# Attention for one query per head over 16 heads: a pair's maximum and exponentials between two Ks, three transfers joined, spare products ahead of every V

## The chip, the core and the metric

The kernel runs on one core of a Trainium2 chip. The metric is device time in microseconds (us). Three runs of the kernel before took 316.85, 317.12 and 317.5 us; their median is 317.12 us. The engines are named as in the profile: PE (matrix products), PEld (its weight loads), DVE (vector), ACT (scalar functions), POOL (GpSimd) and SP, which issues nearly all transfers here.

## The reference

```python
B, H, Sq, Sk, D = 1, 16, 1, 8192, 256          # q, k, v in bfloat16

def reference(q, k, v):
    scale = q.shape[-1] ** -0.5
    scores = jnp.einsum("bhqd,bhkd->bhqk", q, k) * scale
    p = _softmax(scores, axis=-1)
    return jnp.einsum("bhqk,bhkd->bhqd", p, v)
```

There is one query row for each head, so K and V (67 MB each) are read once and used once. The output is 16 rows of 256 numbers.

## The kernel before

**Tiles.** The heads are taken two at a time, as eight pairs, 0 to 7. K of a pair is a tile of 128 partitions (64 for each head) with 128 keys of 256 numbers in each partition, 8.39 MB; V of a pair has the same form. `kbuf` holds two Ks, `vbuf` one V. K5, say, is the K of pair 5. A "side" is one half of a K, 64 keys in each partition (`SIDES`, `HJ`).

**The order of the transfers** is written out by hand in `ORDER` and issued by SP in one queue (L138). A name with `+` is the second part of a K (keys 64 to 127) or of a V (from key 70, `VC`). V7 comes in five pieces (`CUTS`). Ahead of a K, SP waits until DVE and POOL are done with the K two before it (semaphores `kd` and `tp`). Ahead of a V, or of a part from key 70, it waits until PE is done with all of the V before (`pr`), and ahead of a V's first part until PE is done with the first 70 keys of the V before (`pa`). A wait on SP holds everything behind it in the list.

**Scores.** In each side, POOL multiplies 24 of the 64 keys by the query, three keys at a time ("a group", L215), into one of two buffers `prod`; ACT sums each group (L452) and thereby frees the buffer. DVE multiplies and sums the other 40 keys by itself (L252). A K has 16 groups, eight in each side. Semaphore `tp` counts groups multiplied, `sp` groups summed (it starts at 2).

**Maximum and exponentials.** `top` (L234, DVE) takes the maximum of a pair's scores in each partition, `turned` (L292, PE) turns it into a row, `xmax` (L238, DVE) takes the maximum of each head, `spread` (L295, PE) hands it to all partitions, and `expo` (L406 and L411, ACT) makes the exponentials `E`. In the kernel before, DVE and ACT do this for pair h-1 after the first side of pair h (`s == 0`), and at the end, for pair 7, after its last side.

**V.** PE then multiplies E with V, two keys in one product (`doubles`, L317): 35 products for keys 0 to 69, 29 for the rest; for V7, 14 products for keys 70 to 97 and 60 small ones (L386) for the last 30 keys, as they land. `total` (L305) sums the exponentials. ACT copies the sums out (`collect`, L425), PE gathers the parts (`gather`, L342), ACT divides and writes them (`final`, L432). Each round h of PE's loop does V of pair h-1 first, then `turned` and `spread` of pair h, then `gather` of pair h-1. `keep_running` (L331) makes 12 products whose result nobody uses; before, it stands behind `spread` in rounds 6 and 7, in place of the query product that the other rounds have there.

What the change touches, and what calls it:

Of the kernel before, what the change touches and what calls it, by code (L numbers as in the profile page):

```python
# [6 lines left out]
ACT = mybir.ActivationFunctionType  # L7
# [5 lines left out]
NPL = 24  # L13
GRP = 3
CH = 8
SIDES = 2
ORDER = "k0 k0+ k1 v0 k2 v1 k3 v2 k4 v3 k5 v4 k6 k6+ k7 v5 v5+ k7+ v6 v6+ v7"
CUTS = (0, 70, 98, 114, 124)
LAST_PAIRED = 98
SPARES = 6  # L20
STRIP = 64
BLK = 32
ROWS = 98
AHEAD = {"sp": 2, "fin": 1, "rc": 2, "pr": 2, "pv": 2}


def bass_standalone__mha_softmax__decode_kernel(nc: bass.Bass, q: bass.AP, k: bass.AP, v: bass.AP, out: bass.AP):
    B, H, Sq, D = q.shape
# [23 lines left out]
    with contextlib.ExitStack() as ctx:  # L52
# [46 lines left out]
        spare = ps("spare", [P, 512])  # L99

        stream = []
        parts = {name: (0, HJ if name[0] == "k" else VC) for name in ("k0", "k6", "k7", "v5", "v6")}
        for name in ORDER.split():
            kind, n = name[0], int(name[1])
            if name == f"v{LAST}":
                for a, b in zip(CUTS, CUTS[1:] + (J,)):
                    stream.append((kind, n, a, b, "v" if a < VC else "vb" if a < LP else f"w{a}"))
            elif name.endswith("+"):
                stream.append((kind, n, HJ if kind == "k" else VC, J, "vb" if kind == "v" else "k7b" if n == LAST else "kb"))
            else:  # L110
                stream.append((kind, n, *parts.get(name, (0, J)), f"k{n % 2}" if kind == "k" else "v"))

# [10 lines left out]
        @(lambda f: f(nc.sync))  # L123
        def _(sp):
            for kind, n, a, b, name in stream:
                if kind == "k" and n >= 2 and a == 0:
                    sp.wait_ge(sem("kd"), (n - 1) * NC)
                    sp.wait_ge(sem("tp"), (n - 1) * NG)
                elif kind == "v" and n >= 1 and a in (0, VC):
                    sp.wait_ge(*((sem("pa"), n) if b <= VC else (sem("pr"), n + 2)))  # L130
                if kind == "k" and n == 0 and a == HJ:
                    for late in ("k1", "kb", "k7b", "vb"):
                        sp.nop().then_inc(sem(late), 16)
                if kind == "k":
                    buf = kbuf[:, n % 2 * J * D :]
                else:
                    buf = vbuf
                sp.dma_start(buf[:, a * D : b * D], src(k if kind == "k" else v, n)[:, a * D : b * D]).then_inc(  # L138
                    sem(name), 16
                )  # L140
            sp.wait_ge(sem(stream[-1][-1]), 16)
            sp.wait_ge(sem("fin"), LAST + 1)
            flat = out.rearrange("b (n two) s d -> two (b n s) d", two=2)
            rows = qo[:, :].rearrange("t (n d) -> t n d", d=D)
            sp.dma_start(flat[:, 0:LAST, :], rows[:, 0:LAST, :]).then_inc(sem("o"), 16)
            sp.wait_ge(sem("fin"), LAST + 3)
            sp.dma_start(flat[:, LAST:NP, :], rows[:, LAST:NP, :]).then_inc(sem("o"), 16)
            sp.wait_ge(sem("o"), 32)
            sp.nop()
# [4 lines left out]
            e.wait_ge(sem("k1"), (h + 1) // 2 * 16 + 16)  # L154

        def side_wait(e, h, s):
            side, sides = h * SIDES + s, NP * SIDES
            e.wait_ge(sem("kb"), ((side + sides - 1) // sides + (side + 3) // sides) * 16 + 16)  # L158
            e.wait_ge(sem("k7b"), (side + 1) // sides * 16 + 16)

        @(lambda f: f(nc.gpsimd))
        def _(pool):
# [42 lines left out]

            with pool.Fori(0, NP) as h:
                par = pool.snap(h % 2)
                with pool.Fori(0, SIDES) as s:
                    k_waits(pool, h)
                    side_wait(pool, h, s)  # L210
                    pool.nop().then_inc(sem("turn"), 1)
                    with pool.Fori(0, SG // 2) as i:  # L212
                        for b in range(2):
                            pool.wait_ge(sem("sp"), h * NG + s * SG + i * 2 + (b + 1))  # L214
                            pool.tensor_tensor(  # L215
                                out=prod[:, b * GRP * D : (b + 1) * GRP * D].rearrange("p (b d) -> p b d", b=GRP),
                                in0=kbuf[
                                    :, ds(par * (J * D) + s * (HJ * D) + i * (2 * GRP * D) + b * (GRP * D), GRP * D)
                                ].rearrange("p (b d) -> p b d", b=GRP),
                                in1=q_now[:, ds(par * D, D)].rearrange("p (b d) -> p b d", b=1).to_broadcast([P, GRP, D]),  # L220
                                op=ALU.mult,
                            ).then_inc(sem("tp"), 1)

        @(lambda f: f(nc.vector))
        def _(dve):
# [15 lines left out]

            with dve.Fori(0, NP + 1) as h:
                par = dve.snap(h % 2)
                with dve.Fori(0, SIDES) as s:
                    with dve.If(h < NP):
                        k_waits(dve, h)
                        side_wait(dve, h, s)
                        dve.nop().then_inc(sem("turn"), 1)
                        with dve.Fori(0, SC) as c:
                            for b in range(CH):  # L250
                                col = kbuf[:, ds(par * (J * D) + s * (HJ * D) + c * (CH * D) + (NPL + b) * D, D)]
                                ins = dve.scalar_tensor_tensor(  # L252
                                    out=col,
                                    in0=col,
                                    scalar=SCALE,
                                    in1=qrow[:, ds(par * 512, D)],
                                    op0=ALU.mult,
                                    op1=ALU.mult,
                                    accum_out=S[:, ds(par * J + s * HJ + c * CH + (NPL + b), 1)],
                                )  # L260
                            ins.then_inc(sem("kd"), 1)
                    with dve.If(s == 0):
                        with dve.If(h > 0):
                            top(h, 1)
                            xmax(h, 1)
                        with dve.If(h > 1):
                            recips(h, 2)
            recips(NP, 1)
            dve.wait_ge(sem("pv"), NP + 3)
            dve.wait_ge(sem("rc"), NP + 2)  # L270
# [10 lines left out]
        def _(pe):  # L281
# [75 lines left out]
            with pe.Fori(0, NP + 1) as h:  # L357
                par = pe.snap(h % 2)
                with pe.If(h > 0):
                    pe.wait_ge(sem("ex"), h)  # L360
                    pe.wait_ge(sem("v"), h * 16)
                    doubles(0, VC).then_inc(sem("pa"), 1)
                    pe.wait_ge(sem("vb"), (h // (NP - 2) + h // LAST + h // NP) * 16 + 16)
                    doubles(VC, LP)
                    with pe.If(h < NP):
                        doubles(LP, J)
                    total(h)
                with pe.If(h < NP):
# [3 lines left out]
                    spread()  # L372
                    with pe.If(h < NP - 2):
                        qcast(back(h, -2), par)
                    with pe.Else():
                        keep_running()
                with pe.If(h > 0):
                    pe.wait_ge(sem("cm"), h)
                    pe.wait_ge(sem("fin"), h)
# [17 lines left out]
        def _(act):  # L397
# [45 lines left out]
            with act.Fori(0, NP + 1) as h:  # L443
                par = act.snap(h % 2)
                other = act.snap((h + 1) % 2)
                with act.Fori(0, SIDES) as s:
                    with act.If(h < NP):
                        with act.Fori(0, SG) as i:  # L448
                            act.wait_ge(sem("tp"), h * NG + s * SG + i + 1)
                            for b in range(GRP):  # L450
                                part = prod[:, ds(i % 2 * (GRP * D) + b * D, D)]
                                ins = act.activation(  # L452
                                    out=part,
                                    in_=part,
                                    func=ACT.Copy,
                                    scale=SCALE,
                                    accum_out=S[:, ds(par * J + s * HJ + i * GRP + b, 1)],
                                )
                            ins.then_inc(sem("sp"), 1)
                    with act.If(s == 0):  # L460
                        with act.If(h > 0):
                            expo(h, 1)
                        with act.If(h < LAST):
                            q_copy(h + 1, other)
                        with act.If(h > 1):
                            collect(h, 2)
                    with act.If(s == 1):
                        with act.If(h > 1):
                            final(h, 2)
            collect(NP, 1)  # L470
            act.wait_ge(sem("pv"), NP + 3)
            act.wait_ge(sem("rc"), NP + 2)
# [32 lines left out]
```

## Time and profile before

| what | us |
|---|---|
| median of three runs | 317.12 |
| the profiled execution, its own time | 317.33 |
| its span (first to last instruction) | 315.9 |
| DVE, POOL, ACT, PE busy | 225.6, 209.5, 194.6, 97.5 |
| share of 16 transfer engines' span in use by SP's queue | 98.8% |

The span is what the page and all views of the trace show. The execution's own time is 1.43 us longer, for what lies around the span. Times in the views count from the start of the span. "Waits" and "chain" rows give a start, a length and the engine and line; a timeline row gives start, length, engine, line, operation, `out<-in`, how many instructions were merged, and in brackets the idle time ahead of it and who ended it.

### The profile page before, as it was taken

What the parts mean: (1) busy time and instruction counts of PE and PEld (TensorE: products, weight loads), DVE (VectorE), ACT (ScalarE), POOL (GpSimd) and SP (SyncE); (2) the same over time, 40 slices, a digit from 0 to 9 for tenths busy, and PEclk for the clock granted to TensorE, in tenths of its full rate; (3) what the DMA queues carried; (4) which work ended last, traced back from release to release, by engine and by line L of the source; (5) the groups of instructions that cost most, each with busy time, mean ns of one, the idle gap of its engine ahead of it and who ended that gap; (6) DMA issues with size and microseconds to landing.
All of it is one profiled execution on the core that took longest, in us unless ns stands there. A gap on an engine that the chain in (4) does not pass through costs nothing.

```text
span 315.9 us, 7077 instructions
## 1 busy us (share of the span) xinstructions
PE 97.5 (31%) x701; PEld 45.5 (14%) x701; DVE 225.6 (71%) x1305; ACT 194.6 (62%) x840; POOL 209.5 (66%) x145
## 2 busy tenths in 40 slices
PE   0000000191003900048000490005700355285796
PEld 0000000041001400014000240002300122032344
DVE  0198989695596936969279692896989698969300
ACT  2066677766368653696437964468677967686541
POOL 3188888865586836858368582786888588868300
PEclk9999999997555885559755587555965558759599
DMA  8999999999999999999999999999999999999996
GB/s 333 415 448 465 465 398 398 523 407 398 398 523 407 398 398 498 432 398 398 506 423 398 398 514 415 398 398 465 398 465 398 436 446 446 411 436 421 437 429 260
DMA packets 3640, 134.26 MB, mean 425 GB/s; under 512 B 406, under 2 KB 438, under 8 KB 694
## 3 DMA queue, kind: packets, MB, share of 16 engines
q1 hardware_dynamic: 3620, 134.23, 98.8%
q8 instruction: 1, 0.02, 0.0%
q14 instruction: 1, 0.01, 0.0%
q10 hardware_dynamic: 18, 0.01, 0.0%
HBM read 134.23 MB, written 0.01 MB: 425 GB/s over the span
## 4 chain that ended last, share of the span: by engine, by line
DMA 54%; POOL 16%; ACT 10%; issue 6%; ACTq 6%; PE 4%; POOLq 3%; SPq 0%
DMA kbuf<-in_k_dram 32%; DMA vbuf<-in_v_dram 22%; POOL prod L215 16%; ACT prod L452 8%; ACTq L452 4%; PE acc L317 3%; POOLq L215 2%; ACTq L448 2%; SPq L138 0%; ACT E L411 0%; ACT comb L425 0%; PE ob L386 0%; POOLq L214 0%; POOLq L158 0%; POOLq L212 0%
## 5 line engine op out<-in xcount | busy, mean ns | idle before, releaser
L252 DVE SCALAR_TENSOR_TENSOR kbuf<-kbuf,qrow x640 | 219.9, 417 | 65.1 <-issue 65.1
L215 POOL TENSOR_TENSOR prod<-kbuf,q_now 128x768 f32 x128 | 207.0, 1639 | 83.6 <-ACT prod L452 46.3
L452 ACT ACTIVATE prod<-prod x384 | 155.3, 405 | 103.6 <-POOL prod L215 86.6
L317 PE MATMUL acc<-vbuf,E 128*64 128x512 bf16 x497 | 70.4, 448 | 17.5 <-DMA vbuf<-in_v_dram 14.5
L452 ACT ACTIVATION_READ_ACCUMULATOR prod<-prod x384 | 71.6, 186 | 0.0
L292 PE MATMUL mx<-ident,small 128*1 128x128 f32 x16 | 4.5, 380 | 176.7 <-DVE small L234 176.7
L252 DVE DVE_READ_ACCUMULATOR kbuf<-kbuf,qrow x640 | 52.8, 83 | 0.0
L317 PEld LDWEIGHTS acc<-vbuf,E 128*64 128x64 bf16 x497 | 32.2, 129 | 55.0 <-issue 21.1
L292 PEld LDWEIGHTS mx<-ident,small 128*1 128x1 f32 x16 | 0.7, 81 | 178.1 <-DVE small L234 177.9
L411 ACT ACTIVATE E<-S,negb 64x128 bf16 x16 | 13.8, 864 | 1.6 <-ACT negb L406 1.4
L342 PE MATMUL ob<-comb,small 98*2 98x128 f32 x64 | 6.9, 356 | 16.8 <-ACT comb L425 16.7
L228 DVE RECIPROCAL small<-tot 34x1 f32 (+1 forms) x8 | 1.3, 159 | 9.7 <-PE tot L305 9.6
L238 DVE TENSOR_REDUCE small<-mx 1x2 f32<-1x128 f32 x8 | 2.2, 279 | 8.3 <-PE mx L292 8.3
L411 ACT ACTIVATION_READ_ACCUMULATOR E<-S,negb 64x1 f32 x16 | 7.9, 493 | 0.0
L425 ACT ACTIVATE comb<-acc 98x512 f32<-98x512 f32 x8 | 4.7, 593 | 5.0 <-PE tot L305 5.0
L331 PE MATMUL spare<-ident 128*128 128x512 bf16 x24 | 7.6, 486 | 0.0
L342 PEld LDWEIGHTS ob<-comb,small 98*2 98x2 f32 x64 | 2.6, 96 | 20.2 <-ACT comb L425 18.9
L432 ACT ACTIVATE qo<-ob,small 2x128 f32 x14 | 4.9, 352 | 1.0 <-PE ob L342 0.9
L295 PE MATMUL mx<-small 1*128 1x2 f32 x16 | 4.4, 344 | 3.0 <-DVE small L238 3.0
L295 PEld LDWEIGHTS mx<-small 1*128 1x128 f32 x16 | 3.8, 289 | 6.8 <-DVE small L238 6.8
L234 DVE TENSOR_REDUCE small<-S 128x1 f32 x8 | 2.3, 282 | 2.8 <-ACT prod L452 2.8
L406 ACT ACTIVATE negb<-mx 128x2 f32<-128x2 f32 x8 | 1.3, 166 | 4.3 <-PE mx L295 4.2
(25 smaller groups left out, 21.4 us busy)
## 6 DMA issues: line engine op xcount, KB each, us to landing
kbuf<-in_k_dram SPq DMA_DIRECT2D x6, 4096.0 KB, 27.9
vbuf<-in_v_dram SPq DMA_DIRECT2D x3, 4480.0 KB, 23.6
vbuf<-in_v_dram SPq DMA_DIRECT2D x2, 3712.0 KB, 28.9
vbuf<-in_v_dram SPq DMA_DIRECT2D x1, 1792.0 KB, 8.6
vbuf<-in_v_dram SPq DMA_DIRECT2D x1, 1024.0 KB, 10.7
vbuf<-in_v_dram SPq DMA_DIRECT2D x1, 640.0 KB, 11.8
vbuf<-in_v_dram SPq DMA_DIRECT2D x1, 256.0 KB, 11.9
kbuf<-in_k_dram SPq DMA_DIRECT2D x5, 43.5
```

Of the source, the lines that this page charges most:

```text
L215: pool.tensor_tensor(out=prod[:, b * GRP * D : (b + 1) * GRP * D].rearrange("p (b d) -> p b d", b=GRP), in0=kbuf[:, ds(par * (J * D) + s * ...
L252: ins = dve.scalar_tensor_tensor(out=col, in0=col, scalar=SCALE, in1=qrow[:, ds(par * 512, D)], op0=ALU.mult, op1=ALU.mult, accum_out=S[:, ...
L292: pe.matmul(mx[0:1, 0:P], lhsT=m[:, :], rhs=ident[:, :], start=True, stop=True).then_inc(sem("mT"), 1)
L295: pe.matmul(sm, lhsT=ones[0:1, :].to_broadcast([1, P]), rhs=g[:, :], start=True, stop=True,).then_inc(sem("bc"), 1)
L317: ins = pe.matmul(acc[at : at + STRIP, :], lhsT=E[:, x : x + STRIP], rhs=vbuf[:, j * D : (j + 2) * D], start=(j < 4), stop=(j >= J - 4), s ...
L331: pe.matmul(spare[:, :].rearrange("p (b x) -> p b x", x=2 * P), lhsT=flat[:, n * P : (n + 1) * P], rhs=flat.rearrange("p (b x) -> p b x", ...
L342: ins = pe.matmul(ob[row : row + 2, 0:HW], lhsT=sel[:, 2 * n : 2 * n + 2], rhs=comb[:, n * D + a : n * D + a + HW], start=(n == 0), stop=( ...
L411: ins = act.activation(out=E[rows, 0 : 2 * J].rearrange("p (b two i t) -> p b i two t", b=J // BLK, two=2, t=2)[:, :, :, :, x], in_=S[rows ...
L425: act.activation(out=comb[:, :], in_=acc[0:ROWS, :], func=ACT.Copy).then_inc(sem("cm"), 1)
L432: ins = act.activation(out=qo[:, ds(i * D + a, HW)], in_=ob[row : row + 2, 0:HW], func=ACT.Copy, scale=recip[row : row + 2, ds(i, 1)],)
L448: with act.Fori(0, SG) as i:
L452: ins = act.activation(out=part, in_=part, func=ACT.Copy, scale=SCALE, accum_out=S[:, ds(par * J + s * HJ + i * GRP + b, 1)],)
```

## The change

Four things are done. **The transfers:** K0, K6 and V5 come whole and V5 comes ahead of K7's first part; 22 input transfers of K and V stand in place of 25. **The maximum and the exponentials** of pair h-1 are taken by DVE and ACT before their first instruction on K of pair h, in the place where one K ends and the next begins; `collect` of pair h-2 goes ahead of it on ACT. ACT's loop over 16 groups is one loop now. **The spare products** leave their place behind `spread` and go to the head of every round of PE that has a V: PE waits until the pair's groups are all summed (for V6 in round 7: until five groups of K7 are), makes 12 spare products, and then waits for the exponentials and for V. **POOL and DVE** wait for K once in each pair and only for K7's second part in between.

```diff
-ORDER = "k0 k0+ k1 v0 k2 v1 k3 v2 k4 v3 k5 v4 k6 k6+ k7 v5 v5+ k7+ v6 v6+ v7"
+ORDER = "k0 k1 v0 k2 v1 k3 v2 k4 v3 k5 v4 k6 v5 k7 k7+ v6 v6+ v7"
...
+SPARES_AT = 5
...
-        parts = {name: (0, HJ if name[0] == "k" else VC) for name in ("k0", "k6", "k7", "v5", "v6")}
+        parts = {name: (0, HJ if name[0] == "k" else VC) for name in ("k7", "v6")}
...
             with dve.Fori(0, NP + 1) as h:
                 par = dve.snap(h % 2)
-                with dve.Fori(0, SIDES) as s:
-                    with dve.If(h < NP):
-                        k_waits(dve, h)
+                with dve.If(h > 0):
+                    top(h, 1)
+                    xmax(h, 1)
+                with dve.If(h > 1):
+                    recips(h, 2)
+                with dve.If(h < NP):
+                    k_waits(dve, h)
+                    dve.nop().then_inc(sem("turn"), 1)
+                    with dve.Fori(0, SIDES) as s:
                         side_wait(dve, h, s)
...
-                    with dve.If(s == 0):
-                        with dve.If(h > 0):
-                            top(h, 1)
-                            xmax(h, 1)
-                        with dve.If(h > 1):
-                            recips(h, 2)
...
                 with pe.If(h > 0):
+                    pe.wait_ge(sem("sp"), h * NG + h % NP // LAST * SPARES_AT + AHEAD["sp"])
+                    pe.nop().then_inc(sem("turn"), 1)
+                    keep_running()
                     pe.wait_ge(sem("ex"), h)
                     pe.wait_ge(sem("v"), h * 16)
...
                     with pe.If(h < NP - 2):
                         qcast(back(h, -2), par)
-                    with pe.Else():
-                        keep_running()
...
                 other = act.snap((h + 1) % 2)
...
+                with act.If(h > 1):
+                    collect(h, 2)
+                with act.If(h > 0):
+                    expo(h, 1)
+                with act.If(h < LAST):
+                    q_copy(h + 1, other)
+                with act.If(h < NP):
+                    with act.Fori(0, NG) as i:
+                        first = act.snap(par * J + i // SG * (HJ - NPL) + i * GRP)
+                        act.wait_ge(sem("tp"), h * NG + i + 1)
...
+                with act.If(h > 1):
+                    final(h, 2)
```

How SP's list reads around K6 and K7. Of the kernel before (128x16384 is one half of a K, 128x17920 the first 70 keys of a V, 128x14848 the rest):

```order
L138 DMA vbuf<-in_v_dram 128x32768 [waits pr]
L138 DMA kbuf<-in_k_dram 128x16384 [waits tp,kd]
L138 DMA kbuf<-in_k_dram 128x16384
L138 DMA kbuf<-in_k_dram 128x16384 [waits tp,kd]
L138 DMA vbuf<-in_v_dram 128x17920 [waits pa]
L138 DMA vbuf<-in_v_dram 128x14848 [waits pr]
L138 DMA kbuf<-in_k_dram 128x16384
```

And of the changed kernel, from V4 to V6:

```order
L136 DMA vbuf<-in_v_dram 128x32768 [waits pr]
L136 DMA kbuf<-in_k_dram 128x32768 [waits tp,kd]
L136 DMA vbuf<-in_v_dram 128x32768 [waits pr]
L136 DMA kbuf<-in_k_dram 128x16384 [waits tp,kd]
L136 DMA kbuf<-in_k_dram 128x16384
L136 DMA vbuf<-in_v_dram 128x17920 [waits pa]
```

K6's two halves have become one transfer, V5's two parts one that waits for all of V4, and K7's two halves now follow each other behind V5.

How one round of PE reads from `spread` to `gather`, before:

```order
L295 MATMUL mx<-small 128x2 [waits g]
L373 COMPARE_AND_BRANCH
L283 ISA x2
L283 MATMUL qrow<-qo,which 128x256
L373 UNCONDITIONAL_BRANCH
L329 UNCONDITIONAL_BRANCH
L331 MATMUL spare<-ident 128x512 x2
L329 REGISTER_ALU
L329 COMPARE_AND_BRANCH
L375 UNCONDITIONAL_BRANCH
L377 COMPARE_AND_BRANCH
L342 MATMUL ob<-comb,small 2x128 [waits fin,cm]
```

And from its head to V's second part in the changed kernel:

```order
L359 COMPARE_AND_BRANCH
L360 ISA
L329 UNCONDITIONAL_BRANCH [waits sp]
L331 MATMUL spare<-ident 128x512 x2
L329 REGISTER_ALU
L329 COMPARE_AND_BRANCH
L317 MATMUL acc<-vbuf,E 64x512 [waits v,ex]
L317 MATMUL acc<-vbuf,E 64x512 x34
L366 ISA
L317 MATMUL acc<-vbuf,E 64x512 [waits vb]
```

The spare products (a loop of six rounds with two products) have gone from between `spread` and `gather` to ahead of the first product with V, behind a wait for `sp`; in the last round, that of V7, they come after `spread` of pair 7 and `gather` of pair 6.

More of the change, by code (lines that the diff above doesn't have):

```diff
@@ L108, in bass_standalone__mha_softmax__decode_kernel @@
             elif name.endswith("+"):
-                stream.append((kind, n, HJ if kind == "k" else VC, J, "vb" if kind == "v" else "k7b" if n == LAST else "kb"))
+                stream.append((kind, n, HJ if kind == "k" else VC, J, f"{kind}b"))
             else:
@@ L130, in _ @@
                     sp.wait_ge(*((sem("pa"), n) if b <= VC else (sem("pr"), n + 2)))
-                if kind == "k" and n == 0 and a == HJ:
-                    for late in ("k1", "kb", "k7b", "vb"):
-                        sp.nop().then_inc(sem(late), 16)
                 if kind == "k":
@@ L140, in _ @@
                 )
+                if kind == "k" and n == 0:
+                    for late in ("k1", "kb", "vb"):
+                        sp.nop().then_inc(sem(late), 16)
             sp.wait_ge(sem(stream[-1][-1]), 16)
@@ L156, in side_wait @@
         def side_wait(e, h, s):
-            side, sides = h * SIDES + s, NP * SIDES
-            e.wait_ge(sem("kb"), ((side + sides - 1) // sides + (side + 3) // sides) * 16 + 16)
-            e.wait_ge(sem("k7b"), (side + 1) // sides * 16 + 16)
+            e.wait_ge(sem("kb"), (h * SIDES + s + 1) // (NP * SIDES) * 16 + 16)
         @(lambda f: f(nc.gpsimd))
@@ L207, in _ @@
                 par = pool.snap(h % 2)
+                k_waits(pool, h)
+                pool.nop().then_inc(sem("turn"), 1)
                 with pool.Fori(0, SIDES) as s:
-                    k_waits(pool, h)
                     side_wait(pool, h, s)
@@ L362, in _ @@
                     doubles(0, VC).then_inc(sem("pa"), 1)
-                    pe.wait_ge(sem("vb"), (h // (NP - 2) + h // LAST + h // NP) * 16 + 16)
+                    pe.wait_ge(sem("vb"), (h // LAST + h // NP) * 16 + 16)
                     doubles(VC, LP)
@@ L445, in _ @@
                 other = act.snap((h + 1) % 2)
[L446 to L469, printed above, removed]
+                with act.If(h > 1):
[8 more added lines that the diff above has]
+                        act.wait_ge(sem("tp"), h * NG + i + 1)
+                        for b in range(GRP):
+                            part = prod[:, ds(i % 2 * (GRP * D) + b * D, D)]
+                            ins = act.activation(
+                                out=part,
+                                in_=part,
+                                func=ACT.Copy,
+                                scale=SCALE,
+                                accum_out=S[:, ds(first + b, 1)],
+                            )
+                        ins.then_inc(sem("sp"), 1)
+                with act.If(h > 1):
+                    final(h, 2)
             collect(NP, 1)
```

## The prediction

> **What bounds the kernel now.** I read the page first, then the chain of waits, then the timeline of the last 40 us by engine. The page says that the transfer queue is in use all the time:
>
> ```profile
> span 315.9 us, 7077 instructions
> DMA  8999999999999999999999999999999999999996
> q1 hardware_dynamic: 3620, 134.23, 98.8%
> ```
>
> The chain of waits (start, length, what) gives the landings:
>
> ```profile
> 0.74 12.23 DMA kbuf<-in_k_dram
> ...
> 75.98 43.52 DMA kbuf<-in_k_dram
> ...
> 152.62 44.60 DMA kbuf<-in_k_dram
> 197.24 0.23 POOLq L158
> ...
> 198.52 1.63 POOL prod L215
> ...
> 231.18 33.95 DMA vbuf<-in_v_dram
> ...
> 270.33 23.94 DMA vbuf<-in_v_dram
> 294.32 6.04 PE acc L317 x28
> ...
> 301.47 11.78 DMA vbuf<-in_v_dram
> ```
>
> K0's first half lands at 12.97, K3 at 119.50, K5 at 197.22, V5's second part at 265.13, V6's at 294.27, the last piece but one of V7 at 313.25. Between K3 and K5 lie four whole tiles in 77.72 us, 19.43 us each. So the stream never stops, and the middle of the kernel can't go faster unless the stream does. What ends the kernel is read from the tail of PE's timeline:
>
> ```profile
> 277.20 0.59 PE L292 MATMUL mx<-ident,small 128*1 128x128 f32 x2 [6.91 <-DVE small L234]
> 278.15 0.58 PE L295 MATMUL mx<-small 1*128 1x2 f32 x2 [0.37 <-DVE small L238]
> 278.67 4.89 PE L331 MATMUL spare<-ident 128*128 128x512 bf16 x12
> ...
> 285.50 4.07 PE L317 MATMUL acc<-vbuf,E 128*64 128x512 bf16 x35 [1.40 <-DMA vbuf<-in_v_dram]
> 294.32 6.25 PE L317 MATMUL acc<-vbuf,E 128*64 128x512 bf16 x29 [4.75 <-DMA vbuf<-in_v_dram]
> ...
> 300.50 0.38 PE L292 MATMUL mx<-ident,small 128*1 128x128 f32 x2
> 301.25 0.38 PE L295 MATMUL mx<-small 1*128 1x2 f32 x2 [0.37 <-DVE small L238]
> 301.61 2.75 PE L331 MATMUL spare<-ident 128*128 128x512 bf16 x12
> 304.45 0.61 PE L342 MATMUL ob<-comb,small 98*2 98x128 f32 x8
> 305.14 5.79 PE L317 MATMUL acc<-vbuf,E 128*64 128x512 bf16 x49
> ...
> 311.65 0.60 PE L342 MATMUL ob<-comb,small 98*2 98x128 f32 x8 [0.69 <-ACT comb L425]
> 312.08 2.23 PE L386 MATMUL ob<-vbuf,E 128*2 128x128 bf16 x60
> ```
>
> V7's first 70 keys land 70/128 of 19.43 us after V6, at 294.27 + 10.63 = 304.90, and PE begins V7 at 305.14, having worked without a stop since 300.50. Its last product ends at 314.31, 1.06 us after V7's last piece but one (the last, 4 of 128 keys, lands 0.61 behind that, at 313.86): PE and the stream end together, and PE has no slack from `turned` (300.50) on. What PE waited for there is seen on DVE and ACT:
>
> ```profile
> 297.10 0.29 DVE L234 TENSOR_REDUCE small<-S 128x1 f32 x1 [2.79 <-ACT prod L452]
> 300.92 0.28 DVE L238 TENSOR_REDUCE small<-mx 1x2 f32<-1x128 f32 x1 [3.54 <-PE mx L292]
> ```
>
> ```profile
> 296.71 0.19 ACT L452 ACTIVATION_READ_ACCUMULATOR prod<-prod  x1
> ...
> 301.67 0.17 ACT L406 ACTIVATE negb<-mx 128x2 f32<-128x2 f32 x1 [4.15 <-PE mx L295]
> ...
> 302.91 0.86 ACT L411 ACTIVATE E<-S,negb 64x128 bf16 x1
> ```
>
> ACT is done with K7 at 296.90 and DVE has the maximum at 297.39; `turned` could run at 297.44 and runs at 300.50, since PE is still at V6's second part. K7's scores have 3.06 us of slack, no more.
>
> **The change part by part.** *Joined transfers.* From 265.13 to 294.27 three transfers of 12.58 MB (K7's second half, V6's two parts) took 29.14 us; 1.5 whole tiles take 29.15. A cut costs nothing, so joining gains nothing.
>
> The Trainium skill ("DMA: Bandwidth & Descriptors", section "Anatomy of one DMA — SWDGE (gpsimd) path") puts a fixed cost of about 2.0 us on a DMA, mostly its completion; three DMAs fewer would be 6 us of stream less by it, an estimate. The page fits it to another issue path, and the rows disagree for transfers that stand in SP's queue: 29.14 against 29.15.
>
> *K6 whole.* It lands two tiles after K5, at 197.22 + 38.86 = 236.08. K5's scores run without a stop from 198.52 for about 31 us, to 229.8; the gap's maximum and exponentials end by 234. So K6 starts at its landing, and POOL 1.28 us behind it (197.24 to 198.52): 237.36. Before, POOL went on to K6's first half at 230.8, right behind K5. The pace of POOL and ACT:
>
> ```profile
> 44.75 3.23 POOL L215 TENSOR_TENSOR prod<-kbuf,q_now 128x768 f32 x2 [0.53 <-ACT prod L452]
> ...
> 59.80 3.23 POOL L215 TENSOR_TENSOR prod<-kbuf,q_now 128x768 f32 x2 [0.53 <-ACT prod L452]
> ```
>
> ```profile
> 230.78 1.64 POOL L215 TENSOR_TENSOR prod<-kbuf,q_now 128x768 f32 x1 [0.53 <-ACT prod L452]
> ...
> 252.09 3.23 POOL L215 TENSOR_TENSOR prod<-kbuf,q_now 128x768 f32 x2 [2.71 <-ACT prod L452]
> ...
> 291.96 3.23 POOL L215 TENSOR_TENSOR prod<-kbuf,q_now 128x768 f32 x2 [0.53 <-ACT prod L452]
> ```
>
> ```profile
> 250.37 0.42 ACT L452 ACTIVATE prod<-prod  x1
> ```
>
> ```profile
> 230.70:263.00 32.30, 7.84 (x48) 3.37 (x48) 28.14 (x163) 24.11 (x105) 25.88 (x16) 0.58 0.98 424
> ```
>
> Two groups take 3.76 us (15.05 over four steps), and from the start of the last two on POOL to their end on ACT it is 296.90 − 291.96 = 4.94. K6's 16 groups: 237.36 + 7 × 3.76 + 4.94 = 268.6. DVE, with 28.1 us of work in a K (the last row, a window over K6: length, then PE, PEld, DVE, ACT, POOL busy), is done before that.
>
> *The gap.* DVE's maximum starts 0.20 after ACT's last group, `turned` 0.34 after that (0.29 and a signal of 0.05, as from 301.20 to 301.25), `spread` starts 0.75 later (0.95 at the low clock), takes 0.38 (0.58), and from there to the end of the exponentials it is 0.04 + 2.10 (301.67 to 303.77). Sum at the low clock: 0.20 + 0.34 + 0.95 + 0.58 + 2.14 = 4.2 us, in which ACT sums no group; POOL gets two groups ahead, no more, for want of buffers. V5 has landed 19.43 us after K6, at 255.5, and takes PE at most 13.4 us (64 products, 0.21 each at the low clock by the 6.04 for the second part of V6), so PE is free by 268.9. In pairs 0 to 5 this gap hides behind the stream: 31.2 + 4.2 us of scores for each K against 38.86 of transfers. Without that cover it costs 4.2 a pair, and behind K6 there is none.
>
> *K7.* It has landed by 275.0. ACT's first group starts at 268.6 + 4.2 = 272.8; POOL's third group 1.72 us after (250.37 to 252.09): 274.5; six steps of 3.76 to the last two, 297.1; plus 4.94: **302.0**, against 296.90 before, 5.1 us later. 3.06 of it is slack. `turned` moves from 300.50 to 302.0 + 0.54 = 302.5 or 302.6: **+2.1 us**.
>
> *The spare products of V7.* They were between `spread` and `gather`; now they are behind both, and still ahead of V7, since round 7 has to end first. From `turned` to V7 PE makes the same instructions in another order: 305.14 − 300.50 = 4.64 us, ending at 307.2. The exponentials (4.64 includes their 3.27) are hidden by it, as V7's landing is now. Behind V7's start nothing has slack: 49 products in 5.79 without a stop, copy, `gather`, 60 small ones; their end goes from 314.31 to 316.4, and the span from 315.9 to **318.0**, if the clock is as before.
>
> *The clock.* Rows of windows (stretch and its length, busy time of PE, PEld, DVE, ACT, POOL, clock, transfers):
>
> ```profile
> 278.60:283.60 5.00, 5.00 (x15) 1.78 (x17) 3.04 (x17) 4.70 (x17) 3.23 (x2) 0.56 1.03 444
> 293.30:300.10 6.80, 5.78 (x28) 2.49 (x30) 1.30 (x7) 3.22 (x14) 1.90 (x2) 0.50 1.02 437
> 300.10:316.00 15.90, 12.83 (x148) 6.74 (x144) 0.94 (x4) 4.17 (x10) 0.00 (x0) 1.00 0.82 343
> ```
>
> After idle 4.75 us the clock was halved, and it came back after 5.8 us of products; 12 spares took 4.89 at a clock of 0.56 and 2.75 at full. In the change PE has from V6's end (300.4, or 298 if V6 runs at full clock) to the spares (304.5) only some 1.7 us of small work. That is close to the idle stretch that halved the clock and more than the 1.40 that didn't, so I take a halved clock as somewhat likelier than not. It costs up to 2.14 in the spares and, if it lasts into V7, up to 1 more (0.21 against 0.12 us for a product): 0 to 3 us, and I take 1.0.
>
> The Trainium skill ("TensorE: Matmul & The Clock Gate", section "What's actually happening") halves the clock after an idle window of about 3.4 us and restores it after a busy one, with windows that run freely. By that alone, with V6 done at 300.4, no whole window of the stretch is empty, the spares run at full clock, and the span is 318.0; the trace shows no stretch as thin as this, so it can't say.
>
> *The other spares* cost nothing: those of pairs 1 to 6 run when a K is done, long ahead of their V, and PE is idle there. V6's wait for five groups of K7 (the fifth starts on POOL at 274.5 + 3.76 and ends on ACT 4.94 − 1.6 later, 281.6) and take 4.89: V6 starts near 286.5 where it was 285.50 and its first part ends near 290.6 (before 289.57). Only then can V7's first transfer be issued; the queue has work until 294.27, a cover of 3.7 us. *K0 whole* lands at 12.97 + 9.71 = 22.7 where its first half came at 12.97. Its products end on POOL at 22.7 + 1.3 + 7 × 3.76 + 3.23 = 53.5, and K2 can be issued. The queue holds K1 and V0 until 61.5, a cover of 8 us. K3, V1 and the rest stand behind that on SP and have more.
>
> Sum: 315.9 + 2.1 + 1.0 = 319.0 of span. The profiled execution lay 1.43 above its span and 0.21 above the median: 319.0 + 1.43 − 0.21 = **320.2**.
>
> **Rivals.** *No change, 317.1:* the scores of K7 end by 300.0, within the slack. That needs 2 us less than my 65 us of scores and gap from 237.36 on. For it: POOL's idle 0.53 in each step might shrink in ACT's single loop. Against: the step is set by POOL's operation, a signal, ACT's sums and a signal, and none of these is changed:
>
> ```profile
> L215 POOL TENSOR_TENSOR prod<-kbuf,q_now 128x768 f32 x128 | 207.0, 1639 | 83.6 <-ACT prod L452 46.3
> ```
>
> *Faster, 314:* a cut costs the stream what the first transfer needs beyond its data, 12.23 − 9.71 = 2.5. Two cuts fewer ahead of K6's landing (K0's and K6's own) bring it and K7's end 5 us forward, K7's scores end at 297.0 as before, V6 lands three cuts or 7.5 earlier and frees PE by 293; `turned` runs at 297.5 in place of 300.50, 3 us sooner, and all behind it. It decides from a cut of about 1.4 us on (two make up 2.1 and the 0.6 to be told apart). Against it: 29.14 for three transfers, 29.15 by whole tiles.
>
> The Trainium skill's 2.0 us for a DMA (the section named above) would make it 4 us forward for K6, `turned` at 298.5 and a time of about 315; the rows are against it as told.
>
> *The stream runs dry, 322:* V6's spares come so late or slow that V7's first transfer is issued after the queue is empty. It takes over from a delay of 3.7 us less the 2.5 that a first transfer needs beyond its 9.71 (12.23 from issue to landing), so 1.2 us beyond my 290.6; each us more is one later for V7, and it tops the 2.1 only when it is larger than that.
>
> **How the numbers follow.** Forecast 0.80 (slower), dry stream 0.05 (slower), no change 0.10, faster 0.05. A measurement can tell about 0.2% (0.6 us) from no change. Faster 0.05, same 0.10, slower 0.85. The range: 318.0 is the sum at full clock (319.2) less 1.2 for the pace of K6 and K7, 322.2 is a halved clock through spares and into V7 (319.2 + 3.0); the two other cases of 0.15 are left out.
>
> **What would show it.** Right: POOL idle from about 228 to 237; K7's last group on ACT near 302; `turned` of pair 7 directly behind it and not behind V6; V7's products from 307 on or later, with no wait for a landing; the last landing still near 313.9, with PE working 2 us or more behind it; GB/s unchanged. Wrong: K7's scores done by 300; spares at 2.75 (then 319.2); a hole in the transfers near 294 or 61; the last landing earlier than 313.

## The result, and the profile after

The changed kernel takes 321.93 us (median of four runs, 321.37 to 322.3) where the kernel before takes 317.16 on the same chip. The ratio is 1.0152, with a 95% interval from 1.0139 to 1.0164: slower by 4.8 us. Forecast was 320.2, in a range from 318.0 to 322.2. The profiled execution took 321.93. Of all executions told of below, one was in a slow state (325.95 us at a mean clock of 0.62, where the same kernel otherwise had 0.75 to 0.79), and that kernel's ratio leaves it out.

The page of the changed kernel:

```profile
span 320.5 us, 7035 instructions
DMA  9999999999999999999999999999999999999990
q1 hardware_dynamic: 3188, 134.23, 97.3%
L331 PE MATMUL spare<-ident 128*128 128x512 bf16 x96 | 39.6, 597 | 11.7 <-ACT prod L459 10.4
```

The transfers fill every slice but the last, which is new: the stream is over at 313.8 (SP issues the first output at 313.78, on the last piece of V7), 5 us before PE's last product. There are 96 spare products where there were 24.

K6's landing in the chain of waits:

```profile
190.97 44.74 DMA kbuf<-in_k_dram
```

POOL around K6 and K7 (start, length, and in brackets the idle time ahead):

```profile
224.88 3.24 POOL L215 TENSOR_TENSOR prod<-kbuf,q_now 128x768 f32 x2 [0.57 <-ACT prod L459]
236.99 3.23 POOL L215 TENSOR_TENSOR prod<-kbuf,q_now 128x768 f32 x2 [8.88 <-issue]
...
267.54 3.23 POOL L215 TENSOR_TENSOR prod<-kbuf,q_now 128x768 f32 x2 [0.59 <-ACT prod L459]
274.68 3.24 POOL L215 TENSOR_TENSOR prod<-kbuf,q_now 128x768 f32 x2 [3.90 <-ACT prod L459]
```

K6 has landed whole at 235.71. POOL stands idle for 8.88 us from K5's end until just after that, and for 3.90 behind K7's first two groups, while DVE, PE and ACT do the maximum and the exponentials of pair 6 in the gap. DVE's maximum of pair 7 shows when K7's scores were done, and PE's tail what stands behind it:

```profile
302.79 0.29 DVE L234 TENSOR_REDUCE small<-S 128x1 f32 x1 [3.27 <-ACT prod L459]
```

```profile
293.96 3.42 PE L317 MATMUL acc<-vbuf,E 128*64 128x512 bf16 x29 [3.33 <-DMA vbuf<-in_v_dram]
297.01 0.20 PE L305 MATMUL tot<-lsum,half 128*34 128x1 f32 x2
303.13 0.58 PE L292 MATMUL mx<-ident,small 128*1 128x128 f32 x2 [5.74 <-DVE small L234]
304.08 0.58 PE L295 MATMUL mx<-small 1*128 1x2 f32 x2 [0.37 <-DVE small L238]
304.60 1.02 PE L342 MATMUL ob<-comb,small 98*2 98x128 f32 x8
305.73 4.63 PE L331 MATMUL spare<-ident 128*128 128x512 bf16 x12
310.29 5.58 PE L317 MATMUL acc<-vbuf,E 128*64 128x512 bf16 x49
...
317.03 1.85 PE L387 MATMUL ob<-vbuf,E 128*2 128x128 bf16 x60
```

PE is done with V6 at 297.21 and waits 5.74 us, now for DVE's maximum. `turned` of pair 7 runs at 303.13 (before: 300.50). V7 begins at 310.29 (before: 305.14), with no wait for its landing. And the clock, in windows (stretch and its length, busy PE, PEld, DVE, ACT, POOL, clock, transfers):

```profile
297.20:303.10 5.90, 0.19 (x2) 0.00 (x0) 2.61 (x15) 4.41 (x20) 3.23 (x2) 0.97 0.96 413
303.10:310.29 7.19, 6.67 (x24) 2.51 (x24) 0.44 (x2) 3.33 (x9) 0.00 (x0) 0.55 0.94 397
310.29:316.00 5.71, 5.62 (x52) 2.99 (x51) 0.05 (x1) 0.05 (x1) 0.00 (x0) 1.00 0.44 173
```

The clock was halved just before PE went on, and it came back just before V7 began. The end of PE's last product moved from 314.31 to 318.88, by 4.57 us, in three pieces. `turned` is 2.63 later. From `turned` to V7 it takes 7.16 in place of 4.64, 2.52 more, 1.88 of that in the spares (4.63 against 2.75). From V7's start to the end it takes 8.59 in place of 9.17, 0.58 less: the landings that PE used to keep pace with are long past.

### The profile page after: what moved, and what is told of

It is laid out like the page before. It is cut to its first block, busy times and chain, and to the rows that moved or that the text cites. A ratio compares the mean times of both kernels' runs of the same rounds, so it can differ in the third digit from the quotient of the medians.

```text
span 320.5 us, 7035 instructions
## 1 busy us (share of the span) xinstructions
PE 124.9 (39%) x773; PEld 58.0 (18%) x773; DVE 225.5 (70%) x1305; ACT 195.7 (61%) x840; POOL 209.7 (65%) x145
## 4 chain that ended last, share of the span: by engine, by line
POOL 26%; DMA 21%; ACT 17%; issue 12%; ACTq 11%; PE 6%; POOLq 5%; DVE 1%; DVEq 0%; SPq 0%
POOL prod L215 26%; DMA kbuf<-in_k_dram 21%; ACT prod L459 16%; ACTq L459 8%; POOLq L215 4%; ACTq L454 2%; PE acc L317 2%; PE spare L331 1%; PE mx L292 1%; PE mx L295 1%; ACT E L412 1%; POOLq L214 1%; DVE small L234 1%; DVE small L238 1%; PE ob L387 1%
## 5 line engine op out<-in xcount | busy, mean ns | idle before, releaser
L317 PE MATMUL acc<-vbuf,E 128*64 128x512 bf16 x497 | 65.3, 426 | 55.9 <-DMA vbuf<-in_v_dram 55.9
L317 PEld LDWEIGHTS acc<-vbuf,E 128*64 128x64 bf16 x497 | 34.1, 122 | 88.3 <-issue 67.1
L331 PE MATMUL spare<-ident 128*128 128x512 bf16 x96 | 39.6, 597 | 11.7 <-ACT prod L459 10.4
L331 PEld LDWEIGHTS spare<-ident 128*128 128x128 bf16 x96 | 12.7, 139 | 37.1 <-issue 36.7
L342 PE MATMUL ob<-comb,small 98*2 98x128 f32 x64 | 7.7, 391 | 0.7 <-ACT comb L426 0.7
```

The source lines that it names most:

```text
L317: ins = pe.matmul(acc[at : at + STRIP, :], lhsT=E[:, x : x + STRIP], rhs=vbuf[:, j * D : (j + 2) * D], start=(j < 4), stop=(j >= J - 4), s ...
L331: pe.matmul(spare[:, :].rearrange("p (b x) -> p b x", x=2 * P), lhsT=flat[:, n * P : (n + 1) * P], rhs=flat.rearrange("p (b x) -> p b x", ...
L342: ins = pe.matmul(ob[row : row + 2, 0:HW], lhsT=sel[:, 2 * n : 2 * n + 2], rhs=comb[:, n * D + a : n * D + a + HW], start=(n == 0), stop=( ...
```

## The experiments

Twelve kernels were run. The ratio is always to the kernel before, on the same chip.

| what runs | median, us | ratio (95%) |
|---|---|---|
| the change | 321.93 | 1.0152 (1.0139 to 1.0164) |
| the change, K6 and V5 in parts, old order | 321.65 | 1.0131 (1.0107 to 1.0154) |
| before, K6 and V5 whole | 321.99 | 1.0152 (1.0135 to 1.0169) |
| the change, 24 spares ahead of K7's maximum | 321.02 | 1.0132 (1.0110 to 1.0153) |
| the change without V7's spares | 320.23 | 1.0092 (1.0075 to 1.0109) |
| before with the gap and K0 whole | 320.80 | 1.0119 (1.0078 to 1.0159) |
| the change, K6 in two parts | 318.42 | 1.0040 (1.0019 to 1.0062) |
| before, V5 whole and ahead of K7 | 319.11 | 1.0070 (1.0047 to 1.0094) |
| before, K0 whole | 322.68 | 1.0144 (1.0092 to 1.0195) |
| before, spares ahead of V | 318.48 | 1.0054 (1.0033 to 1.0074) |
| the change, 24 spares and 4 more | 320.19 | 1.0097 (1.0078 to 1.0115) |
| the change, K0 in halves | 322.08 | 1.0129 (1.0079 to 1.0180) |
| the change, K6 in two parts, V6's spares later | 317.23 | 0.9987 (0.9966 to 1.0009) |

### K6 and V5 whole, alone

```diff
-ORDER = "k0 k0+ k1 v0 k2 v1 k3 v2 k4 v3 k5 v4 k6 k6+ k7 v5 v5+ k7+ v6 v6+ v7"
+ORDER = "k0 k0+ k1 v0 k2 v1 k3 v2 k4 v3 k5 v4 k6 v5 k7 k7+ v6 v6+ v7"
```

> The kernel before with one thing of the change: K6 and V5 whole and V5 ahead of K7's two halves; maximum, exponentials and spares in their old places, K0 in halves. Theory: scores of K6 start at 237.4 in place of 230.8, the pair K6 and K7 takes 66.1 us as before, K7's last group ends near 303.5, `turned` at 304.0 in place of 300.5; V7 4.6 (full clock) to 7.2 (half clock) behind it; time 320.7 to 323.3, as slow as the change. Rival (the gap or the spares cost it): 317 to 318.

Measured: 321.99 us, inside what was expected, and as slow as the whole change. POOL and PE in this kernel:

```profile
237.22 3.23 POOL L215 TENSOR_TENSOR prod<-kbuf,q_now 128x768 f32 x2 [7.07 <-issue]
```

```profile
303.56 0.58 PE L292 MATMUL mx<-ident,small 128*1 128x128 f32 x2 [5.94 <-DVE small L234]
...
305.03 4.78 PE L331 MATMUL spare<-ident 128*128 128x512 bf16 x12
...
310.27 5.58 PE L317 MATMUL acc<-vbuf,E 128*64 128x512 bf16 x49
```

K6 starts at 237.22, `turned` of pair 7 waits for DVE until 303.56, and the spares run at the halved clock though they stand in their old place, ahead of `gather`. So neither the gap nor the spares' new place is needed for the loss. How much of it is V5's new place ahead of K7 is asked further down.

### K6 and V5 in parts again, in the change

```diff
-ORDER = "k0 k1 v0 k2 v1 k3 v2 k4 v3 k5 v4 k6 v5 k7 k7+ v6 v6+ v7"
+ORDER = "k0 k1 v0 k2 v1 k3 v2 k4 v3 k5 v4 k6 k6+ k7 v5 v5+ k7+ v6 v6+ v7"
...
-        parts = {name: (0, HJ if name[0] == "k" else VC) for name in ("k7", "v6")}
+        parts = {name: (0, HJ if name[0] == "k" else VC) for name in ("k6", "k7", "v5", "v6")}
```

> The changed kernel with K6 and V5 in two parts again and in the old order of the stream (K6, K6+, K7, V5, V5+, K7+, V6); the gap, the spares ahead of V and the whole K0 stay. Theory (K6's whole landing starts its scores 6 us later, and that is the loss): POOL starts on K6 by 230, K7's last group on ACT is summed at 297 to 298, `turned` of pair 7 near 298, the spares are over before V7 lands, V7 starts within 1 us of its landing at 304.9; time 317.0 to 318.0. Rival (the gap between two Ks costs more than the interlude in mid-K did): K7 late all the same, 320 or more. Rival (the spares ahead of V are what costs): V7 starts at 307 or later, 319 or more.

Measured: 321.65 us. The theory missed; the time is that of its two rivals. POOL and PE of this kernel:

```profile
228.58 3.23 POOL L217 TENSOR_TENSOR prod<-kbuf,q_now 128x768 f32 x2 [0.59 <-ACT prod L461]
236.11 3.23 POOL L217 TENSOR_TENSOR prod<-kbuf,q_now 128x768 f32 x2 [4.31 <-ACT prod L461]
...
262.81 3.23 POOL L217 TENSOR_TENSOR prod<-kbuf,q_now 128x768 f32 x2 [0.59 <-ACT prod L461]
274.76 3.24 POOL L217 TENSOR_TENSOR prod<-kbuf,q_now 128x768 f32 x2 [8.71 <-ACT prod L461]
```

```profile
264.71 5.11 PE L319 MATMUL acc<-vbuf,E 128*64 128x512 bf16 x29 [3.08 <-DMA vbuf<-in_v_dram]
269.41 0.23 PE L307 MATMUL tot<-lsum,half 128*34 128x1 f32 x2
269.75 0.38 PE L294 MATMUL mx<-ident,small 128*1 128x128 f32 x2
...
303.17 0.38 PE L294 MATMUL mx<-ident,small 128*1 128x128 f32 x2 [4.47 <-DVE small L236]
```

K6 does start early, at 228.58, 8.4 us ahead of the change. But the gap between K5 and K6, which in the change lies inside the wait for K6's landing, now stops POOL for 4.31 us behind K6's first two groups. And behind K7's first two groups POOL waits 8.71 us in place of 3.90, since the maximum of pair 6 needs `turned` on PE, and PE works through its round in order: V5's second part first, which lands at 264.7 in this order of the stream and is done at 269.64. In mid-K7, where the kernel before takes this maximum, that wait is hidden. So K7's scores end as late as with K6 whole (302.64 on ACT against 302.60), by two other waits that happen to add up to the same. Two runs test the wait for PE.

**The gap alone:** the same kernel, and the spares also back in their old place.

```diff
-                    pe.wait_ge(sem("sp"), h * NG + h % NP // LAST * SPARES_AT + AHEAD["sp"])
-                    pe.nop().then_inc(sem("turn"), 1)
-                    keep_running()
                     pe.wait_ge(sem("ex"), h)
...
+                    with pe.Else():
+                        keep_running()
```

> The changed kernel with the transfers of K6 and V5 in parts and in the old order, as in the run before, and also the spare products back behind `spread` in rounds 6 and 7: of the change the gap (and the whole K0) is left. Theory, new after the first runs: with the maximum in the gap, `turned` of pair 6 has to wait until PE is done with V5, whose second part lands at 264.7 when V5 comes behind K7's first half; so ACT starts K7 near 273 and ends it near 302.6, as late as with K6 whole: 320.3 to 322.3. Rival (the spares' new place was what kept the run with the parts slow): 317 to 318.

Measured: 320.80 us, inside the theory's range. The spares' place is not what kept the kernel with the parts slow.

**K6 in two parts, V5 ahead of K7:** this takes away both the wait for the whole K6 and the wait for PE's V5; the gap between K5 and K6 stays.

```diff
-ORDER = "k0 k1 v0 k2 v1 k3 v2 k4 v3 k5 v4 k6 v5 k7 k7+ v6 v6+ v7"
+ORDER = "k0 k1 v0 k2 v1 k3 v2 k4 v3 k5 v4 k6 k6+ v5 k7 k7+ v6 v6+ v7"
```

> The changed kernel with K6 alone cut in two (K6, K6+, then V5 whole, K7, K7+, V6). Theory (two waits of the same length: K6's whole landing, and PE's V5 ahead of pair 6's `turned`; here both are taken away): K6 from 228.6 to 264, V5 lands at 255.1 and PE is done with it by 264 to 266, `turned` of pair 6 at 264.5 to 266, ACT on K7 from 268 to 269.5, K7's end at 298 to 299, V7 at 305 to 306.8: 317.2 to 319.0. Rival (the gap itself, 4.3 us for the pair, is enough to be late): K7's end beyond 301 and 320 or more.

Measured: 318.42 us (ten runs, 317.66 to 320.12), inside the theory's range.

```profile
265.32 0.38 PE L294 MATMUL mx<-ident,small 128*1 128x128 f32 x2
...
277.81 4.68 PE L333 MATMUL spare<-ident 128*128 128x512 bf16 x12 [10.64 <-ACT prod L461]
285.42 5.61 PE L319 MATMUL acc<-vbuf,E 128*64 128x512 bf16 x35 [2.92 <-DMA vbuf<-in_v_dram]
...
299.19 0.38 PE L294 MATMUL mx<-ident,small 128*1 128x128 f32 x2
...
306.13 4.04 PE L319 MATMUL acc<-vbuf,E 128*64 128x512 bf16 x35 [1.79 <-DMA vbuf<-in_v_dram]
```

`turned` of pair 6 runs at 265.32, that of pair 7 right behind V6 at 299.19, as in the kernel before, and V7 waits for its landing again. Within the change, joining K6 costs the difference, from 1.0040 to 1.0152. What is left lies in the stream: V7 begins at 306.13 and not at 305. V6's spares ended at 282.49, V6 landed at 285.4, the clock had been halved again by then, V6's first 35 products took 5.61 in place of 4.07, and V7's first transfer, which waits for them, was issued late (at 291.05, against 289.60 in the kernel before).

**V6's spares one group later** in that kernel:

```diff
-SPARES_AT = 5
+SPARES_AT = 6
```

> The changed kernel with K6 in two parts (V5 ahead of K7), and V6's spare products after six groups of K7 in place of five. Theory (what this kernel still loses is a hole of 1.2 us ahead of V7: the spares were over 2.9 us ahead of V6's landing, the clock was halved again, V6's first 35 products took 5.6 in place of 4.1, and V7's first transfer was issued late): spares at 279.7 to 284.5, V6 from 285.4 at full clock, V7 lands at 304.9 to 305.2; 317.1 to 318.1. Rival (the hole has another cause): 318.3 or more, V7's landing at 306 as in the run with five groups.

Measured: 317.23 us; the ratio is 0.9987 (0.9966 to 1.0009), no difference from the kernel before. The time is the theory's. That V7's landing moved is not shown: the only trace is of the execution that took 325.95 us.

### The order of V5 and K7, alone

```diff
-ORDER = "k0 k0+ k1 v0 k2 v1 k3 v2 k4 v3 k5 v4 k6 k6+ k7 v5 v5+ k7+ v6 v6+ v7"
+ORDER = "k0 k0+ k1 v0 k2 v1 k3 v2 k4 v3 k5 v4 k6 k6+ v5 k7 k7+ v6 v6+ v7"
```

> The kernel before with V5 whole and ahead of K7's two halves; K6 stays in halves, all else as before. Theory (of the transfers only K6's joining costs): K7's first half lands at 264.9 instead of 245, POOL starts K7 at 266.2 in place of 263.4 and ends it 2.8 later, 299.7, just inside the slack that ends at 299.96: 317.0 to 317.7. Rival (the order of V5 and K7 is what made K6 and V5 whole slow): 320 or more.

Measured: 319.11 us, from 317.5 to 320.26. The theory missed by 1.4 and the rival by 0.9. The profiled execution is the fastest of the four (317.5); in it K7's scores end at 299.0, 0.7 earlier than expected, and V7 waits for its landing. What made the other three 1.4 to 2.8 us longer has no trace. With K6 joined too it was 321.99, 2.9 us more. So V5's place ahead of K7 costs something by itself, 0.5 to 0.9% by the interval, and joining K6 the rest.

### K0 whole, alone and taken back

```diff
-ORDER = "k0 k0+ k1 v0 k2 v1 k3 v2 k4 v3 k5 v4 k6 k6+ k7 v5 v5+ k7+ v6 v6+ v7"
+ORDER = "k0 k1 v0 k2 v1 k3 v2 k4 v3 k5 v4 k6 k6+ k7 v5 v5+ k7+ v6 v6+ v7"
```

> The kernel before with K0 whole, all else as before. Theory: K0's scores start at 23.9 in place of 14.4 and K2 is issued at 53.5, with K1 and V0 in the queue until 61.4; the stream doesn't stop and K7's end stays: 317.0 to 317.6. Rival (late K2 leaves a hole in the stream): each us beyond 61.4 is one of time.

Measured: 322.68 us (320.1 to 323.62), 5 us slower than expected. K2 is issued in time, V1 is not. SP's issues and the chain's landing of K3:

```profile
53.89 0.33 SPq L135 DMA_DIRECT2D kbuf<-in_k_dram  x1
81.41 0.33 SPq L135 DMA_DIRECT2D vbuf<-in_v_dram  x1
```

```profile
85.54 37.23 DMA kbuf<-in_k_dram
```

and PE ahead of it:

```profile
67.57 0.59 PE L292 MATMUL mx<-ident,small 128*1 128x128 f32 x2 [64.50 <-DVE small L234]
...
72.67 8.68 PE L317 MATMUL acc<-vbuf,E 128*64 128x512 bf16 x64 [3.33 <-ACT E L411]
```

With the maximum of pair 0 in mid-K1, and that 9.2 us later than before, PE begins V0 at 72.67 though it landed at 61.4, and V1 can be issued only at 81.41. The queue had only K2 left, and that ended at 80.7. K3 then lands at 122.77 in place of 119.50, and the whole stream is 3.27 us late from there. The rival had the hole, but put it down to a late K2; the late one was V1. The other 2 us or so aren't traced to one cause. In the changed kernel the gap takes that maximum 11.5 us earlier:

```profile
56.03 0.59 PE L292 MATMUL mx<-ident,small 128*1 128x128 f32 x2 [53.09 <-DVE small L234]
```

and SP issues V1 at 71.12:

```profile
71.12 0.33 SPq L136 DMA_DIRECT2D vbuf<-in_v_dram  x1
```

So K0 whole should cost nothing there, which the change with K0 in halves tests:

```diff
-ORDER = "k0 k1 v0
+ORDER = "k0 k0+ k1 v0
```

> The changed kernel with K0 in halves again. Theory: K0 whole, which alone made the kernel before slow (V1 was issued at 81.4, after K2 had landed, since the maximum of pair 0 stood in mid-K1), costs nothing together with the gap, where V1 is issued at 71; so with halves nothing is gained: K6 still starts at its landing near 237, K7 ends near 302.6, 320.8 to 322.3. Rival (K0 whole is part of the change's loss): 320 or less.

Measured: 322.08 us, ratio 1.0129 (1.0079 to 1.0180). Nothing is gained; the theory's range holds.

### The spares and the clock

```diff
                 with pe.If(h > 0):
...
-                    keep_running()
+                    with pe.If(h < NP):
+                        keep_running()
...
+                    with pe.If(h == LAST):
+                        keep_running()
+                        keep_running()
                     pe.wait_ge(sem("m"), h + 1)
```

> The changed kernel, with V7's 12 spare products taken from behind `gather` and 24 put ahead of PE's wait for K7's maximum. Theory (of the 4.6 us lost, 2.5 are the halved clock and the spares that stand between K7's maximum and V7): 24 spares from 297.2 to 302.7 keep the clock, `turned` stays at 303.1, V7 starts as soon as the exponentials are there, 3.3 to 3.6 behind it, at 306.4 to 306.8 and at full clock; time 318.0 to 318.8. Rival (V7 is held by something else, or the clock doesn't matter): 320.5 or more.

Measured: 321.02 us, above both bounds of the theory and in the rival's range. The first `+` part alone, V7 without its spares:

> The changed kernel without V7's 12 spare products. Theory: V7 starts at the end of the exponentials, near 306.9, but at the halved clock, which lasts 3.4 to 6.8 us of products (0.21 each in place of 0.12), so that most of the 3.4 us gained are given back: V7's 49 products take 7.3 to 9 us in place of 5.6; time 320.0 to 321.9. Rival (the spares' own time is all of it, the clock none): V7 at 306.9 in 5.6 us, 318.3.

Measured: 320.23 us, inside the theory's range. The tails of the two, first with 24 spares ahead of the maximum, then with none for V7:

```profile
304.23 0.38 PE L292 MATMUL mx<-ident,small 128*1 128x128 f32 x2 [0.44 <-DVE small L234]
...
307.55 7.08 PE L317 MATMUL acc<-vbuf,E 128*64 128x512 bf16 x49 [1.40 <-ACT E L416]
```

```profile
302.94 0.38 PE L292 MATMUL mx<-ident,small 128*1 128x128 f32 x2 [4.03 <-DVE small L234]
...
306.26 7.95 PE L317 MATMUL acc<-vbuf,E 128*64 128x512 bf16 x49 [1.08 <-ACT E L413]
```

In both V7 begins 3.32 us behind `turned`, as soon as the exponentials are there, against 7.16 in the change. Both lose a part again in V7's products, 7.08 and 7.95 against 5.58, since the clock is halved in them (without spares at 0.50 until 311.0). V7 wasn't held by something else, as the rival has it. With 24 spares it was still full up to `gather`, and was halved for the first 3 us of V7 (windows of that kernel; the clock is the third number from the end):

```profile
303.70:307.20 3.50, 1.52 (x13) 0.78 (x12) 0.72 (x3) 2.81 (x8) 0.00 (x0) 1.00 0.90 387
307.55:310.60 3.05, 3.05 (x16) 1.34 (x18) 0.00 (x0) 0.69 (x2) 0.00 (x0) 0.50 0.98 414
```

That is 1.5 us of the miss. Another 1.1 is a stream that was 1.1 us late in this profile (POOL starts K6 at 238.10 in place of 236.99), for which no cause is known. So 4 more spares were put into that wait:

```diff
+                with pe.If(h == LAST):
+                    keep_running(2)
```

> The changed kernel with 24 spare products ahead of PE's wait for K7's maximum and 4 more behind `gather` of pair 6, in PE's wait for the exponentials, in place of the 12. Theory (the clock is what V7's 49 products lose when they start behind a pause): V7 starts when the exponentials end, 3.3 to 3.6 behind `turned`, and now at full clock, 5.6 in place of 7.1 us: 318.9 to 319.9, 1 to 2 us under the kernel with the 24 alone. Rival (the clock has no part): no difference from it, 320.7 or more.

Measured: 320.19 us, 0.3 above the theory's range and 0.5 below the rival's, 0.8 below the kernel with the 24 alone; the intervals of the two ratios just overlap. V7 runs at full clock:

```profile
307.60 1.04 PE L331 MATMUL spare<-ident 128*128 128x512 bf16 x4
309.37 5.56 PE L317 MATMUL acc<-vbuf,E 128*64 128x512 bf16 x49 [0.73 <-ACT E L418]
```

The sign is the theory's: 5.56 in place of 7.08. The size isn't. In this profile the stream was 1.5 us late again (POOL starts K6 at 238.46), and `turned` had to wait for the 24 spares until 305.75, more than a us behind K7's maximum, as V6 had run at the halved clock and ended at 300.35. What the spares give back in V7 they can take ahead of it: with 28 of them the time is that of the kernel without any for V7 (320.23).

**The spares' new place alone**, in the kernel before:

```diff
+                    pe.wait_ge(sem("sp"), h * NG + h % NP // LAST * SPARES_AT + AHEAD["sp"])
+                    pe.nop().then_inc(sem("turn"), 1)
+                    keep_running()
                     pe.wait_ge(sem("ex"), h)
...
-                    with pe.Else():
-                        keep_running()
```

> The kernel before with the spare products alone moved to the head of each round with a V, as in the change. Theory: V6's second part then runs at full clock, `turned` of pair 7 follows K7's end (297.4 to 298), and the spares behind `gather`, at either clock, are over before V7 lands at 304.9: 316.9 to 317.6, no change. Rival (spares ahead of V7 cost by themselves): 319 or more.

Measured: 318.48 us, ratio 1.0054 (1.0033 to 1.0074). The theory said no change and missed by 0.9, and the rival's 319 wasn't reached; it is a small loss.

```profile
282.75 1.02 PE L343 MATMUL ob<-comb,small 98*2 98x128 f32 x8 [3.99 <-ACT comb L427]
283.90 3.70 PE L332 MATMUL spare<-ident 128*128 128x512 bf16 x12
287.53 4.07 PE L318 MATMUL acc<-vbuf,E 128*64 128x512 bf16 x35
294.36 3.42 PE L318 MATMUL acc<-vbuf,E 128*64 128x512 bf16 x29 [2.75 <-DMA vbuf<-in_v_dram]
...
301.65 0.60 PE L343 MATMUL ob<-comb,small 98*2 98x128 f32 x8 [2.81 <-ACT comb L427]
302.75 4.44 PE L332 MATMUL spare<-ident 128*128 128x512 bf16 x12 [0.50 <-issue]
307.12 5.58 PE L318 MATMUL acc<-vbuf,E 128*64 128x512 bf16 x49
```

V6's second part does run in 3.42. But `gather` waits for ACT's copy, the spares stand behind `gather`, and so V6 begins 2 us later than before (287.53 against 285.50) and V7 at 307.12 instead of 305.14.

## Why the prediction was right, and where its sizes were off

**The cause was the one named.** K6 was put at a start of 237.36 on POOL and started at 236.99; K7's last group was put at 302.0 and ended at 302.60 (the maximum starts 0.19 to 0.20 behind it, at 302.79); `turned` was put at 302.5 or 302.6 and ran at 303.13. V7 waited for no landing and the stream kept its pace. K6 and V5 joined, with the gap and the spares left out, give the whole loss (1.0152); V5's new place without K6's joining gives about half of it (1.0070), with a spread that has no explanation; within the change, cutting K6 alone takes most of it away (1.0040).

That the time fell inside the range is partly luck. The top of the range stood for a halved clock in the spares and on into V7, 3.0 us over the sum at full clock. The clock cost 2.5 ahead of V7 and nothing in V7, K7's end came 0.6 later than put down, and the end of the kernel was 0.58 shorter.

**The pace of a K** was taken as unchanged, 3.76 us for two groups. It was 3.82: POOL's idle time in each step is 0.57 to 0.59 where it was 0.53. Over the 13 steps of K6 and K7 that is 0.8 us, most of the error in K7's end (0.60 later than put down, from a start 0.37 earlier). It is in the kernels with ACT's one loop over 16 groups and not in that with K6 whole alone; that the loop's own instructions do it was not tested.

**The clock** was the mis-sized term: 1.0 us was put down for it, as an average over halved and not halved, and it measured 2.5. The step said "somewhat likelier than not"; it was halved in the traces of the change, of K6 whole and of the gap alone. Of the 2.14 named as most for the spares 1.88 came; the rest came in `spread` and `gather`, which the prediction had left at the full clock. By the Trainium skill's window ("TensorE: Matmul & The Clock Gate", section "What's actually happening") as the prediction read it, the spares would have run at full clock; PE was then taken to be done with V6 at 300.4, though the prediction also named 298 for a V6 at full clock. It was done at 297.2, since V6 did run at full clock (its second part took 3.42 us and not 6.25). The 5.7 us that were empty then are longer than a window of 3.4, and the clock fell 5.5 us into them. The trace agrees with the rule and not with what was put into it.

**The end** was put at the same distance behind V7's start as before; it was 0.58 shorter. Sum: 2.1 + 1.0 forecast, 2.63 + 2.52 − 0.58 measured.

**What was costed at nothing.** Joining saves nothing: the stream ends at 313.8 in the change, where it ended at 313.86. K0 whole was covered in the change, as said, but the reason was incomplete: it is the gap that covers V1, and in the kernel before the same edit costs 5 us. The spares of V6 were called free with a cover of 3.7 us; alone, with those of V7, they cost 1.4 us.

**The rivals.** None came about. The gap was counted at 4.2 us and measured 4.24 on ACT (268.71 to 272.95). But the prediction saw only one of two reasons for a late K7. It noted that PE is free of V5 "by 268.9" and K6 done at 268.6, and took the one for harmless. In the change it is (PE is done with V5 at 263.86). With the parts back in their old order PE's V5 ends at 269.6, and the gap by itself is as late as K6 whole. That, and the cover that the gap gives V1, is why the four edits aren't additive: alone they cost 1.4% for K0, 1.5% for K6 with V5 and 0.5% for the spares, the gap with K0 whole 1.2%, and all together 1.5%.

**What stays open.** Why three of four executions with V5 ahead of K7 took longer than the profiled one; whether the gain of 1.2 us by V6's later spares is V7's landing; and why the stream was a us late in two of the profiles. In those two the edits touch only the spares of V7's round, and POOL's start on K6, long before that round, is late already.

## What to carry to other kernels

When a stream of transfers is never idle, moving work earlier gains nothing in the middle, and an edit that leaves the stream running is priced at the end, by the slack of the chain that finishes there: here 3.06 us, read from one wait (`turned` at 300.50 against 297.44). An edit that stops the stream costs in the middle too, as K0 whole did in the kernel before. A step that is moved to a new place also inherits what stands ahead of it on each engine it uses: the maximum in the gap needs PE, and PE had a V in front of it. Products that only keep the clock up can cost more than they bring: behind K7's maximum, ahead of the last piece of work, 12 of them cost 1.7 us net here (321.93 with them, 320.23 without), and 28 of them in PE's waits gained nothing over leaving them out (320.19).

## What was not expected of the hardware

A halved clock can take some 6 us of work to come back. In the change PE worked for 6.67 of the 7.19 us from 303.10 to 310.29 at a clock of 0.55, while in the kernel before 12 spares after a short pause took 2.75 us at full clock. The same 12 spares took from 2.75 us at full clock to 5.30 in these traces (the longest in the kernel with the gap alone).
